# Decoding float64 weights to float32 on one Trainium2 core: a landing offset and a dtype cast in place of shifts and a sign step

## The chip, the cores and the metric

The kernel runs on one core of a Trainium2 chip. The metric is the device time of one execution in microseconds (us). The kernel before was run three times: 883.78 us is the median, 882.27 the lowest and 884.93 the highest. One further execution was profiled; it took 882.62 us.

## The reference

Two stages follow each other. The first is attention in which a query sees only keys of its own hash bucket; the second is a two-layer network with an ELU between its layers (the names say "moe", but there is one pair of matrices and no routing).

```python
# q, k, v: (4, 8, 768, 64) float32; proj: (64, 6) float32
q_bucket = sum over 6 bits of (q @ proj > 0) * 2**bit      # likewise k_bucket
scores = where(q_bucket == k_bucket, q @ k.T / 8, -1e9)
attn_out = softmax(scores) @ v                             # per batch and head
x = attn_out with the heads side by side                   # (3072, 512)
h = x @ w_in                                               # w_in  (512, 2048)
g = where(h > 0, h, exp(min(h, 0)) - 1)
out = g @ w_out                                            # w_out (2048, 512)
```

The inputs q, k, v and proj are float32. The two weight matrices are float64: a float32 array was multiplied by a float64 scalar. No engine of the core computes in float64, so the kernel has to make float32 numbers out of the 64-bit patterns itself.

## The kernel before, in words

**Stages.** The work is cut into eight chunks, one for each half of the 768 queries of each of the four batches. For a chunk the kernel does the attention of four pairs of heads (24 score tiles of 128 queries by 768 keys, numbered s0, s1, ...) and then the network on the 384 tokens of the chunk (16 blocks of 128 hidden columns). The network of a chunk is interleaved on TensorE with the attention of the next chunk. The first chunk has no network beside it: while its attention runs, the weights are loaded and decoded. That is the part which the change touches.

**Attention of a score tile.** TensorE makes the scores in four matmuls (L840) into one of two double banks of PSUM. VectorE takes them out with a clamp and a running maximum (L863). GpSimd makes the bias of the exponential from the maxima of two tiles (L880). ScalarE computes the exponential in place with its sum (L891). In the first chunk TensorE then transposes the tile in float32 (L907, called flip), ScalarE copies that out (L915), and an fp32 matmul with v follows (L991). In later chunks the normalised tile is split into two f16 halves, on ScalarE (L316) and VectorE (L319), and transposed by DMA.

**Weights.** There are 32 tiles of 128 rows by 512 columns, 16 of w_in and 16 of w_out (function weight_ops, tile i in one(i)). Each tile is loaded from DRAM as 128 rows of 4,096 contiguous bytes (L411). It lands in one of three staging slots in the tile U, or in a fourth at the end of the big tile W, the "raw" slot, which is used for every fourth i. A load waits until the decode before it in that slot is done. The result goes to W, at place i + 1 or i + 2. The decode before:

- ScalarE reads the high word of each float64 as a float32 and multiplies it by 2**-112 (L424, "mul").
- VectorE shifts the result left by three bits (L429) and ors in the low word shifted right by 29 (L430, "or"). Without its sign bit this is the float32.
- TensorE adds the high bf16 halves of the magnitudes over the 128 rows with a matrix of ones (L437), accumulated in PSUM over the 16 tiles of a matrix. The largest column sum bounds every weight, which gives the power of two by which the weights are scaled later (L454 and L455).
- VectorE takes the sign from the high word and ors it in (L446, "sgn"). It waits for L437, since the column sums need magnitudes.

When all 16 tiles of a matrix are decoded and its scale is known, each tile is split into two f16 halves (L472 on ScalarE and L475 on VectorE, through the helpers at L316 and L319). The first matmul of the network (L1083) needs that of w_in.

**Order.** A planner (class Plan) gives each step an engine, an estimated duration, a due time and its dependencies, plays the steps through, and emits every engine's instructions in the order that comes out. On the chip each engine and each DMA queue keeps to that order, so a waiting instruction holds what stands behind it. The loads stand on SP's queue, in one row with the loads of q, k and v, the DMA transposes of K and O and small copies of the hash bits (K<-zb, O<-zb). Buffers are rings with a fixed number of slots. `met` is the list of earlier users of the part of W where a decoded tile goes: the end of W first serves as staging for two of the pairs of heads (stages 1 and 2: natk, natq and their q and k), as scratch for the squares of v (junk0), and as the raw slot.

```python
met = [u for a, z, users in regions if a < (place + 1) * SL and place * SL < z for u in users]
if (place + 1) * SL > RAW:
    met += raw_users
...
m = add("A", mul, act(SL) + 40.0, due, [l] + met, use=[t], name=f"w{i}mul")
```

## Time and profile before

| what | value |
| --- | --- |
| median of three runs | 883.78 us (882.27 to 884.93) |
| the profiled execution, its own time | 882.62 us |
| its span, first to last instruction | 880.9 us |
| TensorE (PE) busy in the span | 809.3 us, 92% |
| ScalarE (ACT) busy | 706.3 us, 80% |
| VectorE (DVE) busy | 696.0 us, 79% |
| GpSimd (POOL) busy | 61.9 us, 7% |
| first matmul of the network (L1083) | at 133.9 us |

The profiled execution's own time is 1.72 us more than its span, and 1.16 us less than the median. In the rows of the profile, "PE busy 60.54 (x318)" is the time in which at least one of 318 matmuls ran in that stretch; PEld is the loading of the stationary matrix, which overlaps PE. PEclk is the clock that TensorE was granted, as a share of full speed. "DMA share" is the mean busy share of the 16 DMA engines in the stretch and can come out a little over 1. Names like U, W, natk are tiles of the kernel; L numbers are lines of the kernel before.

### The profile page before, as it was taken

The numbers are of one execution on the slowest core, as the hardware profiler recorded it, in microseconds if no ns is written. First come the engines' busy times: TensorE is split into PE (matmuls) and PEld (weight loads), VectorE is DVE, ScalarE is ACT, GpSimd is POOL, SyncE is SP. The second block draws the span as 40 slices with busy tenths as digits, with TensorE's granted clock in tenths as the row PEclk, the third lists the DMA queues.
The fourth block names the chain that finished last, engine by engine and source line by source line (L and its number), as shares of the span: only waits on it lengthen the run. The fifth ranks groups of instructions, "written<-read, shape, count | busy, mean of one in ns | idle before, by whom it ended". The sixth has DMA issues, their size and how long they took to land. (4 is left out here: it accounts for less than half of the span.)

```text
span 880.9 us, 14721 instructions
## 1 busy us (share of the span) xinstructions
PE 809.3 (92%) x5119; PEld 432.4 (49%) x5119; DVE 696.0 (79%) x1485; ACT 706.3 (80%) x1293; POOL 61.9 (7%) x123
## 2 busy tenths in 40 slices
PE   1676987899999999999999999989999999999997
PEld 0233543444554555545555555545555555555553
DVE  6899999999997777898887777888887777773332
ACT  4567899999988798988888789987987878874443
POOL 1000000000010000000010000000110000000000
PEclk9988899999999999999999999999999999999999
DMA  9967628878896789795977679967976767563001
GB/s 250 286 186 223 195 46 195 167 135 161 142 181 115 139 165 189 166 184 122 191 162 128 121 171 200 189 137 135 170 163 122 134 115 145 103 100 51 36 0 36
DMA packets 367466, 128.98 MB, mean 146 GB/s; under 512 B 342248, under 2 KB 360352, under 8 KB 367392
## 3 DMA queue, kind: packets, MB, share of 16 engines
q1 hardware_dynamic: 367088, 127.91, 69.4%
q8 instruction: 40, 0.66, 0.3%
q14 instruction: 34, 0.28, 0.1%
q10 hardware_dynamic: 304, 0.13, 0.1%
HBM read 35.65 MB, written 6.29 MB: 48 GB/s over the span
## 5 line engine op out<-in xcount | busy, mean ns | idle before, releaser
L1083 PE MATMUL h<-x,W 128*128 128x384 f16 x1536 | 310.6, 326 | 1.0 <-ACT U L1111 0.9
L1135 PE MATMUL o<-W,U 128*128 128x512 f16 x1152 | 307.4, 379 | 1.6 <-DVE U L319 1.2
L891 ACT ACTIVATE pt<-pt,nb,sg 128x768 f32<-128x768 f32 x192 | 195.3, 1018 | 43.0 <-POOL nb L880 42.9
L1083 PEld LDWEIGHTS <-W 128*128 128x128 f16 x1536 | 148.7, 97 | 137.7 <-issue 6.1
L863 DVE TENSOR_SCALAR_CACHE_REDUCE pt<-s 128x768 f32<-128x768 f32 x180 | 171.4, 952 | 27.1 <-PE s L840 13.5
L319 DVE SCALAR_TENSOR_TENSOR hl<-pt,r,hl 128x768 f16<-128x768 f32 x168 | 167.0, 1014 | 15.2 <-ACT hl L316 15.1
L840 PE MATMUL s<-K,O 128*128 128x384 f16 x720 | 150.3, 332 | 14.2 <-DVE pt L863 13.8
L1135 PEld LDWEIGHTS <-U 128*128 128x128 f16 x1152 | 110.0, 97 | 104.7 <-DVE U L319 3.7
L316 ACT ACTIVATE hl<-pt,r 128x768 f16<-128x768 f32 x168 | 149.1, 926 | 5.8 <-issue 2.1
L840 PEld LDWEIGHTS <-O 128*128 128x128 f16 (+1 forms) x768 | 74.1, 100 | 84.4 <-issue 40.1
L880 POOL TENSOR_SCALAR nb<-m,sg 128x2 f32<-128x2 f32 x96 | 58.6, 611 | 725.2 <-DVE pt L863 580.5
L316 ACT ACTIVATE U<-U,sgg 128x384 f16<-128x384 f32 x128 | 77.9, 609 | 36.4 <-DVE U L1114 36.1
L1114 DVE SCALAR_TENSOR_TENSOR U<-U 128x384 f32<-128x384 f32 x128 | 70.7, 553 | 37.3 <-ACT U L1111 37.2
L319 DVE SCALAR_TENSOR_TENSOR U<-U,sgg 128x384 f16<-128x384 f32 x128 | 78.7, 615 | 25.6 <-ACT U L316 24.6
L1107 ACT ACTIVATE U<-h,ch 128x384 f32<-128x384 f32 x128 | 72.7, 568 | 32.3 <-PE h L1083 30.9
L1021 PE MATMUL av<-PT,vhl 128*64 128x384 f16 x1008 | 90.7, 328 | 7.2 <-DMA PT<-hl 6.3
L1021 PEld LDWEIGHTS <-vhl 128*64 128x64 f16 x1008 | 59.1, 110 | 38.2 <-issue 14.8
L1111 ACT ACTIVATE U<-h,ch 128x384 f32<-128x384 f32 x128 | 72.7, 568 | 0.0
L930 DVE TENSOR_SCALAR r<-sm 128x2 f32<-128x2 f32 x84 | 13.8, 165 | 30.6 <-ACT pt L891 30.4
L891 ACT ACTIVATION_READ_ACCUMULATOR pt<-pt,nb,sg 128x1 f32 x192 | 36.2, 188 | 0.0
L907 PE MATMUL flip<-W,pt 128*128 128x128 f32 x144 | 25.5, 313 | 6.4 <-ACT pt L891 3.0
L907 PEld LDWEIGHTS flip<-W,pt 128*128 128x128 f32 x144 | 19.2, 160 | 18.4 <-ACT PT L915 9.4
(118 smaller groups left out, 572.1 us busy)
## 6 DMA issues: line engine op xcount, KB each, us to landing
U<-in_moe_w_in_dram SPq DMA_DIRECT2D x12, 512.0 KB
vf<-in_v_dram SPq DMA_DIRECT2D x16, 384.0 KB
U<-in_moe_w_out_dram SPq DMA_DIRECT2D x12, 512.0 KB
qst<-in_q_dram SPq DMA_DIRECT2D x30, 192.0 KB
kst<-in_k_dram SPq DMA_DIRECT2D x14, 384.0 KB
out_dram<-W SPq DMA_DIRECT2D x16, 256.0 KB
PT<-hl SPq DMA_TRANSPOSE x168
W<-in_moe_w_in_dram SPq DMA_DIRECT2D x4, 512.0 KB
```

The lines of the kernel that those rows point to most:

```text
L316: nc.scalar.activation(o, x, AF.Copy, scale=s)
L319: nc.vector.scalar_tensor_tensor(o, x, s, hi, ALU.mult, ALU.subtract)
L840: nc.tensor.matmul(s.t[:, y, :HALF], O[x][:rows, j * HC + t, :], K[x][:rows, j * NC + y * HC : j * NC + (y + 1) * HC, :].rearrange("p a b ...
L863: nc.vector.tensor_scalar(pt.t.rearrange("p (n e) -> p n e", n=2), s.t[:, :, :HALF], CLAMP, None, ALU.max, ALU.max, accum_out=m.t[:, y : y ...
L880: nc.gpsimd.tensor_scalar(nb.t, m.t, sg_of(n), -1.0, ALU.mult, ALU.mult)
L891: nc.scalar.activation(pt_.t, pt_.t, AF.Exp, bias=nb.t[:, y : y + 1], scale=sg_of(n), accum_out=sm.t[:, z : z + 1])
L1021: nc.tensor.matmul(av.t[j * D : (j + 1) * D], vs["hl"][p].t[:, j, c, vx, :], PTs[j].t[:, :, px, c, :], start=y == 0, stop=y == 3 * NC - 1,)
L1083: nc.tensor.matmul(h.t, WH[:, g * KT + t, wx, fc * P : (fc + 1) * P], xbuf[NP * ci + t].t[:, xx, :], start=t == 0 and y == 0, stop=t == KT ...
L1107: nc.scalar.activation(e.t, h.t, AF.Exp, scale=c["ch"])
L1111: nc.scalar.activation(hp.t, h.t, AF.Relu, scale=c["ch"])
L1114: nc.vector.scalar_tensor_tensor(e.t, e.t, -1.0, hp.t, ALU.add, ALU.min)
L1135: nc.tensor.matmul(banks[t][:, :DO], g16.t[:, gx, t * P : (t + 1) * P], WH[:, NSI + 1 + f, wx, :], start=f == 0 and y == 0, stop=f == NF - ...
```

## The change

A float64 has one sign bit, 11 exponent bits and 52 bits of mantissa. Its upper 16 bits read as a bf16 have the sign, the exponent without its lowest three bits, and then those three bits and four bits of mantissa as the bf16's mantissa. Cast to f16, which has ten mantissa bits and five exponent bits, the same number has the sign, five exponent bits, the three bits, the four bits and three zeros: for numbers of the size of these weights that is the high half of the float32 but for its last three bits. These and the low half are the next 32 bits of the float64, shifted right by 13. To read these 32 bits as one aligned word the tile must lie two bytes further on in SBUF.

So the load now lands at byte 2 of its slot: `in` is the 2,048 16-bit elements from index 1 on, `top` is every fourth bf16, and `low` is every second 32-bit word. GpSimd clears the target in W (new, "zero"). ScalarE casts `top` from bf16 to f16 into the upper halves of the cleared words (in place of "mul"). VectorE shifts `low` right by 13 and ors it in (the one step left of three). The sign comes along with the cast, so no step waits for TensorE any more.

The bound changes with it, since the tile now has its signs: TensorE multiplies each 128 by 128 block of the high bf16 halves, transposed, with itself, and adds all blocks of a matrix up in one 128 by 128 bank. Its diagonal holds sums of squares. The largest entry of each row is taken (128 by 128 instead of 128 by 512), a matmul with ones adds these up over the partitions, and half the exponent of that is the scale (`squares=True`). TensorE now does four matmuls of 128 columns with four loads of weights per tile, in place of one matmul of 512 columns.

Three small things come along. U gets two more columns and the raw slot two more elements for the offset. The weight's place is met (`met`) by the clearing, and no longer by ScalarE's step. In the first chunk the matmuls that spread the inverse sums ("rows") are planned after the chunk's transposes (`after=flips`), and the step that takes these rows (xw) is named to the planner as the next user of the score tile's ring, so that a slot is kept for it.

```diff
-    U = const.tile([P, 3 * 2 * SL], F32, name="U")
+    U = const.tile([P, 3 * 2 * SL + 2], F32, name="U")
...
-    area["U"] = [U[:, i * 2 * SL : (i + 1) * 2 * SL].bitcast(I32).rearrange("p (n x) -> p n x", x=2) for i in range(3)]
+
+    def staged_at(t, at):
+        halves = t.bitcast(I16)[:, 2 * at : 2 * at + 4 * SL + 4]
+        return {
+            "in": halves[:, 1 : 1 + 4 * SL],
+            "low": t.bitcast(I32)[:, at : at + 2 * SL].rearrange("p (n x) -> p n x", x=2)[:, :, 1],
+            "top": halves[:, 4:].bitcast(BF16).rearrange("p (n x) -> p n x", x=4)[:, :, 0],
+        }
+
+    area["U"] = [staged_at(U, i * 2 * SL) for i in range(3)]
...
-    area["raw"] = [spare(SL, 2).bitcast(I32)]
+    area["raw"] = [staged_at(flat(spare(1, 2 * SL + 2)), 0)]
...
-                nc.sync.dma_start(flat(t.t), src)
+                nc.sync.dma_start(t.t["in"], src)
...
-            def mul():
-                nc.scalar.activation(d, t.t[:, :, 1].bitcast(F32), AF.Copy, scale=2.0**-112)
-
-            m = add("A", mul, act(SL) + 40.0, due, [l] + met, use=[t], name=f"w{i}mul")
-
-            def bits_():
-                nc.vector.tensor_scalar(di, di, 3, None, ALU.logical_shift_left)
-                nc.vector.scalar_tensor_tensor(di, t.t[:, :, 0], 29, di, ALU.logical_shift_right, ALU.bitwise_or)
-
-            s = add("V", bits_, vec(SL, 2.0) + vec(SL) + 70, due, [m], use=[t], name=f"w{i}or")
+            def zero():
+                nc.gpsimd.memset(d, 0.0)
+
+            def top_():
+                nc.scalar.activation(d.bitcast(F16).rearrange("p (n x) -> p n x", x=2)[:, :, 1], t.t["top"], AF.Copy)
+
+            def join():
+                nc.vector.scalar_tensor_tensor(di, t.t["low"], 13, di, ALU.logical_shift_right, ALU.bitwise_or)
+
+            z = add("G", zero, 600.0, due - 4, met, name=f"w{i}zero")
+            m = add("A", top_, act(SL) + 40.0, due, [l, z], use=[t], name=f"w{i}top")
+            s = decoded[i] = add("V", join, vec(SL), due, [m], use=[t], name=f"w{i}or")
 
             def bound():
                 if i in (0, NSI):
-                    acc["t"] = ps_o.tile([P, 512], F32, tag="o2", name="acc")[:, :SL]
-                nc.tensor.matmul(
-                    acc["t"], ones, d.bitcast(BF16).rearrange("p (n t) -> p n t", t=2)[:, :, 1],
-                    start=i in (0, NSI), stop=i in (NSI - 1, NSI + NSO - 1),
-                )
-
-            b = add("P", bound, 220.0, due - 40, [s, cleared] + ([maxes[0]] if i == NSI else []), after=bounds[o][-1:], late=160.0, name=f"w{i}sum")
+                    acc["t"] = ps_o.tile([P, 512], F32, tag="o2", name="acc")[:, :P]
+                high = d.bitcast(BF16).rearrange("p (n t) -> p n t", t=2)[:, :, 1]
+                for x in range(SL // P):
+                    part = high[:, x * P : (x + 1) * P]
+                    nc.tensor.matmul(
+                        acc["t"], part, part, start=i in (0, NSI) and x == 0,
+                        stop=i in (NSI - 1, NSI + NSO - 1) and x == SL // P - 1,
+                    )
+
+            b = add("P", bound, 400.0, due - 40, [s] + ([maxes["seen"]] if i == NSI else []), after=bounds[o][-1:], late=160.0, name=f"w{i}sum")
             bounds[o].append(b)
-
-            def sign():
-                nc.vector.scalar_tensor_tensor(di, t.t[:, :, 1], -(2**31), di, ALU.bitwise_and, ALU.bitwise_or)
-
-            decoded[i] = add("V", sign, vec(SL), due, [b], use=[t], name=f"w{i}sgn")
             if raw:
-                raw_users.append(decoded[i])
+                raw_users.append(s)
             if i in (NSI - 1, NSI + NSO - 1):
+                av = buf("av")
 
                 def reduce_():
                     nc.vector.tensor_reduce(wst["m2"][:, o : o + 1], acc["t"], axis=AX.X, op=ALU.max)
-                    wst["ex", o], wst["sc", o] = exponents(wst["m2"][:, o : o + 1], 1, 2.0**-17, W_TOP, f"w{o}", const)
+
+                def sum_():
+                    av.t = sum_over(wst["m2"][:, o : o + 1], 1)
+
+                def scale():
+                    wst["ex", o], wst["sc", o] = exponents(av.t, 1, 2.0**-34, W_TOP, f"w{o}", const, squares=True)
                     if o == 1:
                         wst["e2"] = const.tile([P, 1], F32, name="we2")
                         nc.vector.tensor_tensor(wst["e2"], wst["ex", 0], wst["ex", 1], ALU.mult)
 
-                maxes[o] = add("V", reduce_, vec(SL) + 5 * TINY, due, [b], name=f"wmax{o}")
+                r = maxes["seen"] = add("V", reduce_, vec(P), due - 40, [b], name=f"wmax{o}")
+                q_ = add("P", sum_, 60.0, due - 40, [r, filled_ones], new=[av], late=160.0, name=f"wsum{o}")
+                maxes[o] = add("V", scale, 6 * TINY, due - 40, [q_], use=[av], name=f"wscale{o}")
...
-            a2 = add("P", spread, 1400.0, due - 1, [a1, cleared], new=[rb], use=[rw], late=160.0, name=f"rows{n}")
+            a2 = add("P", spread, 1400.0, due - 1, [a1, cleared], after=flips, new=[rb], use=[rw], late=160.0, name=f"rows{n}")
-            a3 = add("A", take, act(HALF, 1), due - 1, [a2, vs["scaled"]], new=[xw], use=[rb], name=f"xw{n}")
+            a3 = pt.heir = add("A", take, act(HALF, 1), due - 1, [a2, vs["scaled"]], new=[xw], use=[rb], name=f"xw{n}")
```

The planner is given the new steps, and the engines' orders come out differently. Lines of the changed kernel stand up to 19 further down: L863 is L881 there, L880 is L898, L319 is L329, L720 is L738, L430's place is taken by L440, L437's by L452 and the clearing is L434.

VectorE, from the scale of the third pair of heads (sg) on, before. W<-W,qks is the f16 split of that pair's k and q, zb<-z,pjt its neighbour's hash bits, and the last row is the first score tile's maximum:

```order
L430 SCALAR_TENSOR_TENSOR W<-U,W 128x512
L319 SCALAR_TENSOR_TENSOR W<-W,qks 128x12x64
L319 SCALAR_TENSOR_TENSOR W<-W,qks 128x6x64
L720 TENSOR_SCALAR zb<-z,pjt 128x384
L663 COPY W<-W 128x6x64
L446 SCALAR_TENSOR_TENSOR W<-U,W 128x512
L429 TENSOR_SCALAR W<-W 128x512
L430 SCALAR_TENSOR_TENSOR W<-U,W 128x512
L720 TENSOR_SCALAR zb<-z,pjt 64x384
L772 TENSOR_REDUCE vx_335<-vx 128x1
L446 SCALAR_TENSOR_TENSOR W<-U,W 128x512
L863 TENSOR_SCALAR pt,m<-s 128x768
```

The same place in the changed kernel, from sg up to the second score tile's maximum (pt,m<-so):

```order
L618 SCALAR_TENSOR_TENSOR sg<-ke 128x1
L881 TENSOR_SCALAR pt,m<-s 128x768
L329 SCALAR_TENSOR_TENSOR W<-W,qks 128x12x64
L329 SCALAR_TENSOR_TENSOR W<-W,qks 128x6x64
L738 TENSOR_SCALAR zb<-z,pjt 128x384
L681 COPY W<-W 128x6x64
L440 SCALAR_TENSOR_TENSOR W<-U,W 128x512 x2
L440 SCALAR_TENSOR_TENSOR W<-W 128x512
L738 TENSOR_SCALAR zb<-z,pjt 64x384
L440 SCALAR_TENSOR_TENSOR W<-U,W 128x512
L881 TENSOR_SCALAR pt,m<-so 128x768
```

The first maximum has moved from behind the split, the hash bits and the steps of two to three weight tiles to directly behind the scale, and a weight tile has one row (L440) where it had three.

GpSimd, from the end of the set-up to the end, before. nb is the bias of the exponential, one row for two score tiles:

```order
L337 MEMSET W 128x128
L338 ISA
L338 AFFINE_SELECT W<-W 128x128
L880 TENSOR_SCALAR nb<-m,sg 128x2 x96
L1253 UNCONDITIONAL_BRANCH
```

And in the changed kernel, where L434 clears a weight tile's place:

```order
L347 MEMSET W 128x128
L348 ISA
L348 AFFINE_SELECT W<-W 128x128
L434 MEMSET W 128x512 x22
L898 TENSOR_SCALAR nb<-m,sg 128x2
L434 MEMSET W 128x512
L898 TENSOR_SCALAR nb<-m,sg 128x2 x2
L434 MEMSET W 128x512 x6
L898 TENSOR_SCALAR nb<-m,sg 128x2 x9
L434 MEMSET W 128x512 x3
L898 TENSOR_SCALAR nb<-m,sg 128x2 x84
L1272 UNCONDITIONAL_BRANCH
```

The 32 clearings stand in GpSimd's one queue with the biases: 22 ahead of the first bias, one behind it, six ahead of the fourth, and the last three behind the twelfth.

More of the change, by code (lines that the diff above doesn't have):

```diff
@@ L11 @@
 I32 = mybir.dt.int32
+I16 = mybir.dt.int16
 AF = mybir.ActivationFunctionType
@@ L382, in lsh_attention_moe @@
     filled_ones, cleared, proj_top, projected = begin_ops()
-    wi64 = w_in.bitcast(I32)
-    wo64 = w_out.bitcast(I32)
+    wi64 = w_in.bitcast(I16)
+    wo64 = w_out.bitcast(I16)
     decoded, split_done = {}, {}
@@ L403, in one @@
                 g, kt = i // KT, i % KT
-                src = wi64[kt * P : (kt + 1) * P, 2 * g * SL : 2 * (g + 1) * SL]
+                src = wi64[kt * P : (kt + 1) * P, 4 * g * SL : 4 * (g + 1) * SL]
             else:
@@ L817, in pair_ops @@
         PTs = []
-        filled = []
+        filled, flips = [], []
         sums = buf("sw") if whole else None
@@ L920, in pair_ops @@
                         eye_users.append(fl)
+                        flips.append(fl)
                         ev = add(
```

## The prediction

> **What bounds the kernel now.** I read the page first, for the busy shares and the chain of work that ended last. PE is busy for 92% of the span, and the chain, followed back from the end, is almost all PE, in the two matmuls of the network.
>
> ```profile
> span 880.9 us, 14721 instructions
> PE 809.3 (92%) x5119; PEld 432.4 (49%) x5119; DVE 696.0 (79%) x1485; ACT 706.3 (80%) x1293; POOL 61.9 (7%) x123
> PE o L1135 6%; PE h L1083 6%; PE av L1021 1%; PE s L840 1%; ACT pt L891 0%; DVE W L1189 0%; DVE pt L863 0%; DVE U L319 0%; ACT U L316 0%; ACT U L1107 0%; DVE U L1114 0%; DVE po L1173 0%; ACT U L1111 0%; ACT po L1169 0%; DVE r L930 0%
> ```
>
> An average over stages hides what matters here, so next come the busy times by stretch. I chose the cuts at the points where the limiting engine changes.
>
> ```profile
> core 0: us, PE busy (x) PEld busy (x) DVE busy (x) ACT busy (x) POOL busy (x), PEclk, DMA share, GB/s
> 10.00:30.00 20.00, 8.61 (x41) 2.56 (x41) 18.85 (x52) 11.22 (x24) 0.00 (x0) 1.00 1.05 300
> 30.00:110.00 80.00, 60.54 (x318) 32.98 (x318) 72.81 (x164) 56.35 (x113) 3.73 (x10) 0.89 0.69 206
> 110.00:130.00 20.00, 16.37 (x122) 9.52 (x121) 19.62 (x49) 20.00 (x44) 0.55 (x2) 1.00 0.16 33
> 130.00:240.00 110.00, 98.07 (x637) 51.52 (x634) 104.51 (x217) 108.19 (x196) 8.23 (x15) 1.00 0.81 159
> 240.00:870.00 630.00, 619.84 (x3983) 333.41 (x3982) 475.51 (x990) 502.28 (x905) 46.11 (x69) 1.00 0.69 135
> 870.00:881.00 11.00, 5.41 (x25) 2.09 (x23) 2.41 (x4) 2.72 (x5) 0.00 (x0) 0.91 0.20 72
> ```
>
> From 240 us on PE is busy 619.84 of 630 us: there the kernel is as long as its matmuls. From 110 to 240 us ACT has 128.19 of 130 us, with DVE close behind. From 10 to 110 us DVE is busy 91.66 of 100 us, while PE has 69.15 and ACT 67.57. That is the first chunk's attention with the weights decoded beside it, and only there does DVE alone set the pace. What the first chunk takes less, everything behind it starts sooner; nothing behind it gets shorter by itself.
>
> The decode lies in that stretch: the sign step's last instruction starts at 120.5 us, the network's first matmul at 133.9.
>
> ```profile
> L446 DVE SCALAR_TENSOR_TENSOR W<-U,W x24: 675/686/710, 23.2 to 120.5; 128x512 int32<-128x512 int32 x24
> L1083 PE MATMUL h<-x,W x1536: 322/326/337, 133.9 to 870.3; 128*128 128x384 f16 x192
> ```
>
> **The change part by part.** The groups that the change touches (busy us, mean ns of one, idle before):
>
> ```profile
> L430 DVE SCALAR_TENSOR_TENSOR W<-U,W 128x512 int32<-128x512 int32 x24 | 16.6, 692 | 0.8
> L446 DVE SCALAR_TENSOR_TENSOR W<-U,W 128x512 int32<-128x512 int32 x24 | 16.3, 687 | 1.0 <-PE acc L437 1.0
> L424 ACT ACTIVATE W<-U 128x512 f32<-128x512 f32 x24 | 15.9, 668 | 13.9 <-DMA U<-in_moe_w_in_dram 11.7 <-DMA U<-in_moe_w_out_dram 2.2
> L437 PE MATMUL acc<-W,ones 128*128 128x512 bf16 x32 | 14.4, 470 | 6.3 <-DVE W L430 5.9
> L429 DVE TENSOR_SCALAR W<-W 128x512 int32<-128x512 int32 x32 | 13.5, 422 | 2.2 <-ACT W L424 2.2
> L437 PEld LDWEIGHTS <-ones 128*128 128x128 bf16 x32 | 3.3, 109 | 5.9 <-issue 5.5
> ```
>
> *DVE.* The or step stays as one step of the same form, two words in and one out, 692 ns. The shift (422 ns) and the sign (687 ns) go: 1.11 us for each of 32 tiles, 35.5 us. By stretch (10 to 30, 30 to 110, 110 to 130 us), L446 first and L429 second:
>
> ```profile
> 10.00:30.00 20.00, 2.07 (x3) 1.00 1.05 300
> 30.00:110.00 80.00, 17.42 (x26) 0.89 0.69 206
> 110.00:130.00 20.00, 2.08 (x3) 1.00 0.16 33
> ...
> 10.00:30.00 20.00, 1.66 (x4) 1.00 1.05 300
> 30.00:110.00 80.00, 10.54 (x25) 0.89 0.69 206
> 110.00:130.00 20.00, 1.28 (x3) 1.00 0.16 33
> ```
>
> That is 3.7, 28.0 and 3.4 us. DVE's work from 30 to 110 us falls from 72.8 to 44.9 us, below both PE and ACT, so DVE stops being the bound.
>
> *ACT.* The cast reads 512 elements at the same distance of eight bytes as the multiplication and writes 512, four bytes apart. I take L424's 668 ns: no change. Bounds are 0.1 us less or more on each tile, 3 us either way.
>
> *PE.* Each tile streams 512 columns as before, in four pieces, and loads four stationary blocks where it loaded one. Lower bound: nothing, as loads run beside matmuls (from 240 us on PEld has 333 us inside a PE that is hardly ever idle). Upper bound: three more loads of 109 ns bare, 0.33 us a tile. I take 0.1, nearer to the hidden end: 26 tiles from 30 to 110 us make 2.6 us. Their wait for DVE remains (5.9 us in 12 waits before), but DVE no longer waits for them.
>
> *POOL.* Not in the trace at this size. Two rows bound it:
>
> ```profile
> L329 POOL MEMSET W<- 128x384 f16 x2 | 0.8, 417 | 0.0
> L337 POOL MEMSET W<- 128x128 f32 x1 | 0.2, 209 | 0.1
> ```
>
> From 128 to 384 elements the price rises by 208 ns, so 512 elements cost some 520 ns; 32 of them 16.7 us, on an engine with 3.73 of 80 us in use. The cover is POOL's idleness. What can be late is what is queued behind a clearing that waits: the bias, and behind it the exponential.
>
> ```profile
> 4.28 0.29 POOL L338 TENSOR_SCALAR_AFFINE_SELECT W<-W 128x128 f32<-128x128 f32 x1
> 16.55 1.56 SPq L668 DMA_TRANSPOSE O<-W  x1
> 23.30 1.44 PE L840 MATMUL s<-K,O 128*128 128x384 f16 x4
> 30.35 0.19 ACT L313 ACTIVATION_READ_ACCUMULATOR W<-vf 128x1 f32 x1
> 31.24 0.95 DVE L863 TENSOR_SCALAR_CACHE_REDUCE pt<-s 128x768 f32<-128x768 f32 x1
> ```
>
> The first 18 clearings write unused places and run from 4.6 to 14 us; four more wait for the staging of the second pair of heads, whose last reader is the transpose issued at 16.55 us, so they end by some 22 us if it lands two us later. The first bias needs two score tiles, the first of which is only computed at 23.3 us. The clearing behind the first bias waits for the squares of v, over at 30.5 us, which stand ahead of the first exponential on ACT as well. I cost POOL at nothing.
>
> *Start.* The first score tile is ready at 24.7 us, and its maximum runs at 31.24, behind the split and weight steps that the order shows. Now it stands in front of them; that work must still be done before the second maximum, so I count not the 6.5 us but the 3.7 that DVE loses up to 30 us. The loads set the rest of that stretch (DMA share 1.05).
>
> *Sum.* From 30 to 110 us PE is the next bound, with 60.5 + 2.6 = 63.1 us, and ACT has 56.4. DVE as the bound reached 72.81 of 80 us, 91%, through queues in fixed order. With the same share, PE needs 63.1 / 0.91 = 69.3 us: 10.7 less. From 110 to 240 us ACT is the bound and its work stays: nothing. From 240 us on PE: nothing. Together 3.7 + 10.7 = 14.4 us. The profiled execution took 882.62 us (its span and 1.72), so 868.2; I say 868. That execution lies 1.16 us below the median of the three runs, inside their spread.
>
> *DMA and its landing.* Two bytes off is the part for which no row stands. The tiles go through these issues and two like them for w_out, 32 in all:
>
> ```profile
> U<-in_moe_w_in_dram SPq DMA_DIRECT2D x12, 512.0 KB
> W<-in_moe_w_in_dram SPq DMA_DIRECT2D x4, 512.0 KB
> ```
>
> 32 times 524,288 bytes are 16.8 MB, which at the 300 GB/s of the row with the engines full take 56 us. All DMA work from 10 to 110 us is 20 x 1.05 + 80 x 0.69 = 76 us. I take the landing at its old speed, as rows of 4,096 contiguous bytes stay such rows.
> A rule speaks against that. The Trainium skill (DMA: Bandwidth & Descriptors, "How a descriptor splits into AXI transactions") says that a descriptor is cut at 256-byte boundaries, so one that starts off a boundary needs one transaction more. If it holds for the landing side too, a row makes 17 transactions in place of 16, an estimate of 6% or 3.5 us of DMA time; no run here shows it yet. The sum stays the same by it, and it lowers the chance of the rival below.
>
> **The rivals.**
>
> *The odd landing is slow (slower than before).* If each weight row takes x times as long, the DMA engines have 76 + 56 (x - 1) us of work for that stretch. At x = 1.16 that is the 85 us that my sum leaves of the hundred; at 1.43 the whole gain is gone; at 2 it is 132 us, 32 more than now, and 915 us comes out. For it: ACT waited 11.7 us for w_in even before, and SP's one queue holds the transposes behind the loads. Against it: bytes and contiguous runs are unchanged.
>
> *ACT alone is the bound.* PE ran at 0.89 of its clock from 30 to 110 us; at full clock its 60.5 us are 54, less than ACT's 56.35. At the 98.6% that ACT reaches from 110 to 240 us (128.19 of 130), the stretch takes 57.1 us, 22.9 less, and with the start 26.6: 856 us. Against it: flips and their copies go back and forth between PE and ACT through two banks.
>
> *The queues hold each other up.* If the next bound reaches only 80% of the stretch, since three engines of like load pass each tile on in turn, PE needs 78.9 us: 1.1 plus 3.7 less, 878 us. The waits for it are there:
>
> ```profile
> ACT pt L891 <- POOL nb L880: 10.6, 3, 4.9
> PE acc L437 <- DVE W L430: 5.9, 12, 1.1
> ```
>
> *Clearings hold DVE.* The copies at L640 and L663 move 512 elements in less time than the others (1536 in 545 ns), and 9 of them lie from 10 to 110 us (L640 first, then L663, each from 10 and from 30 us on). If each meets a clearing and waits for it, that is 9 x 0.52 = 4.7 us on a path, 873 us.
>
> ```profile
> L640 DVE COPY K<-K 64x1536 f16<-64x1536 f16 x16 | 8.7, 545 | 1.0 <-DMA K<-natk 1.0
> ...
> 10.00:30.00 20.00, 1.09 (x2) 1.00 1.05 300
> 30.00:110.00 80.00, 1.09 (x2) 0.89 0.69 206
> ...
> 10.00:30.00 20.00, 0.75 (x3) 1.00 1.05 300
> 30.00:110.00 80.00, 0.50 (x2) 0.89 0.69 206
> ```
>
> The Trainium skill (SBUF — State Buffer, "Who interferes with whom") has the rule for it: a VectorE copy in a two-port mode and a GpSimd instruction lock each other out of a shared port pair. No row shows such a meeting yet; the one step of the decode in such a mode, by its 422 ns, is the one removed.
>
> **How the numbers follow.** Forecast 0.62; ACT alone 0.12; queues hold each other up 0.12; clearings 0.05; slow landing 0.09. Same means within 0.3%, 2.6 us, about what a measurement of this kernel tells from no change. The queue case gives 5 us and its worse half can fall inside that: 0.05 for the same. Faster is 0.62 + 0.12 + 0.05 + 0.07 = 0.86, slower 0.09. The range runs from ACT alone, 856, to the queue case, 878; outside lie the slow landing and the worse half of the queue case, with the tail beyond ACT's floor some 0.16.
>
> **What would show it.** Right: DVE has 1.1 us less for each tile, its busy share from 30 us on falls to some 65% until the network begins, PE's rises over 85%, the first h matmul starts near 119.5 us and the stretch behind it keeps its length. Wrong: the cast takes over 0.8 us; L424's 13.9 us of idle time before it, which loads ended, become tens; the bias starts late behind L434; or the first h matmul is early and the end is not, because ACT's stretch to 240 us grew.

## The result, and the profile after

| | median | range | executions |
| --- | --- | --- | --- |
| before | 884.29 us | 882.27 to 887.97 | 13 |
| after | 878.87 us | 874.31 to 881.83 | 13 |

The ratio is 0.9929, 95% interval [0.9909, 0.9949]: 6.3 us faster (4.5 to 8.0), where the prediction said 14.4. The profiled execution of the changed kernel took 875.86 us. Its page and its busy times by stretch, cut as before (columns: stretch, its length, PE, PEld, DVE, ACT, POOL busy, PE's clock, DMA share, GB/s):

```profile
span 874.1 us, 14875 instructions
PE 803.9 (92%) x5217; PEld 433.7 (50%) x5217; DVE 670.7 (77%) x1423; ACT 707.8 (81%) x1293; POOL 81.8 (9%) x155
```

```profile
10.00:30.00 20.00, 6.15 (x36) 2.33 (x39) 17.56 (x52) 8.48 (x17) 5.16 (x11) 1.00 0.82 218
30.00:110.00 80.00, 64.08 (x488) 38.49 (x490) 57.93 (x136) 71.39 (x144) 9.80 (x22) 0.96 0.76 236
110.00:130.00 20.00, 17.79 (x125) 10.12 (x118) 18.70 (x48) 19.84 (x39) 1.74 (x2) 1.00 0.38 92
130.00:240.00 110.00, 96.11 (x606) 48.67 (x604) 98.98 (x204) 103.25 (x187) 10.31 (x13) 0.95 0.79 151
240.00:870.00 630.00, 619.47 (x3976) 333.80 (x3974) 472.41 (x985) 500.68 (x901) 46.05 (x69) 1.00 0.69 133
```

Two things stand out beside the rows of before. From 30 to 110 us VectorE has made room (57.93 of 80 us instead of 72.81) and ScalarE is now the busiest, with 71.39. And from 130 to 240 us, where the changed steps no longer run, all three engines are less busy than before (ScalarE 103.25 instead of 108.19 of 110 us): time is lost there that no engine's work accounts for (the window holds other work than before, as the network starts sooner).

The changed steps themselves, as groups (busy us, mean ns of one, idle before):

```profile
L437 ACT ACTIVATE W<-U 128x512 f16<-128x512 bf16 x24 | 18.6, 785 | 3.6 <-DMA U<-in_moe_w_in_dram 3.1 <-DMA U<-in_moe_w_out_dram 0.5
L440 DVE SCALAR_TENSOR_TENSOR W<-U,W 128x512 int32<-128x512 int32 x24 | 16.3, 686 | 12.8 <-ACT W L437 12.7
L434 POOL MEMSET W<- 128x512 f32 x32 | 15.5, 538 | 15.6 <-DMA O<-W 8.3 <-DVE W L329 5.3 <-ACT W L323 1.1
L452 PE MATMUL acc<-W 128*128 128x128 bf16 x128 | 13.2, 238 | 7.8 <-DVE W L440 7.8
```

The join costs what the or cost, the clearing 538 ns where some 520 were estimated, the products no more than the matmul with the ones (13.2 us for all, 14.4 before). The cast is dearer, 785 ns against 668. The waits of ScalarE for the loads of w_in fell from 11.7 to 3.1 us.

To see where the gain went I follow the first matmuls of the network in the trace. The first h matmul starts at 122.2 us:

```profile
L1102 PE MATMUL h<-x,W x1536: 322/326/527, 122.2 to 863.6; 128*128 128x384 f16 x192
```

It was 133.9, so 11.7 us are gained there. The 193rd h matmul starts the second chunk's share; it came at 241.0 before and comes at 236.2 now, 4.8 earlier. Between these two matmuls PE starts the same 621 matmuls, tile for tile (the rows count those under way at an edge too), yet they take 114.0 us where they took 107.1. The rows for that stretch, of before and of after:

```profile
133.90:241.00 107.10, 95.17 (x624) 50.11 (x622) 101.61 (x212) 105.62 (x193) 6.97 (x14) 1.00 0.81 158
```

```profile
122.20:236.20 114.00, 98.98 (x624) 50.34 (x622) 102.94 (x213) 107.14 (x194) 11.00 (x14) 0.96 0.76 150
```

So 6.9 us are given back behind the point up to which I had counted: PE is busy for 3.8 us more with the same matmuls, at a lower clock, and idle for 3.1 us more. Not all of it is lost for good. Up to the 385th h matmul, the start of the third share and again the same work for PE, the rows of before and of after are:

```profile
133.90:337.50 203.60, 188.80 (x1231) 100.77 (x1229) 180.77 (x378) 185.89 (x338) 14.94 (x26) 1.00 0.81 156
```

```profile
122.20:329.10 206.90, 191.78 (x1231) 100.27 (x1229) 181.30 (x376) 187.19 (x339) 18.34 (x26) 0.98 0.79 152
```

The second share alone takes 92.9 us where it took 96.6, so some 3.6 of the 6.9 us come back in it, and 3.3 are lost.

Another loss lies at the start. After, then before (start us, duration us):

```profile
4.53 8.47 POOL L434 MEMSET W<- 128x512 f32 x18
5.45 0.15 DVE L606 TENSOR_SCALAR qkm<-qkx 128x1 f32<-128x1 f32 x1
5.63 7.39 DVE L608 TENSOR_SCALAR ke<-qkm 128x2 int32<-128x2 int32 x1
13.71 0.17 DVE L608 TENSOR_SCALAR ke<-qkm 128x2 int32<-128x2 int32 x1
```

```profile
5.56 0.17 DVE L590 TENSOR_SCALAR ke<-qkm 128x2 int32<-128x2 int32 x1
```

A VectorE step of two columns, 0.17 us before, now ends at 13.02 us, when the row of 18 clearings ends at 13.00. The step of one column just ahead of it took its usual 0.15 us in the middle of that row, and the same step at 13.71, behind the row, is back at 0.17.

### The profile page after: what moved, and what is told of

Same layout as the page of the kernel before. It is cut to its first block, busy times and chain, and to the rows that moved or that the text cites. A ratio compares the mean times of both kernels' runs of the same rounds, so it can differ in the third digit from the quotient of the medians.

```text
span 874.1 us, 14875 instructions
## 1 busy us (share of the span) xinstructions
PE 803.9 (92%) x5217; PEld 433.7 (50%) x5217; DVE 670.7 (77%) x1423; ACT 707.8 (81%) x1293; POOL 81.8 (9%) x155
## 5 line engine op out<-in xcount | busy, mean ns | idle before, releaser
L881 DVE TENSOR_SCALAR_CACHE_REDUCE pt<-s 128x768 f32<-128x768 f32 x180 | 171.2, 951 | 28.1 <-PE s L858 15.0
L329 DVE SCALAR_TENSOR_TENSOR hl<-pt,r,hl 128x768 f16<-128x768 f32 x168 | 166.0, 1013 | 10.7 <-ACT hl L326 10.6
L1154 PEld LDWEIGHTS <-U 128*128 128x128 f16 x1152 | 110.2, 98 | 112.9 <-ACT U L326 8.2
L898 POOL TENSOR_SCALAR nb<-m,sg 128x2 f32<-128x2 f32 x96 | 63.1, 657 | 683.0 <-DVE pt L881 568.9
L329 DVE SCALAR_TENSOR_TENSOR U<-U,sgg 128x384 f16<-128x384 f32 x128 | 78.6, 614 | 25.9 <-ACT U L326 24.5
L329 DVE SCALAR_TENSOR_TENSOR x<-av,x 128x384 f16<-128x384 f32 x28 | 15.5, 554 | 14.7 <-ACT x L326 14.7
```

The lines of the kernel that those rows point to most:

```text
L329: nc.vector.scalar_tensor_tensor(o, x, s, hi, ALU.mult, ALU.subtract)
L881: nc.vector.tensor_scalar(pt.t.rearrange("p (n e) -> p n e", n=2), s.t[:, :, :HALF], CLAMP, None, ALU.max, ALU.max, accum_out=m.t[:, y : y ...
L898: nc.gpsimd.tensor_scalar(nb.t, m.t, sg_of(n), -1.0, ALU.mult, ALU.mult)
L1154: nc.tensor.matmul(banks[t][:, :DO], g16.t[:, gx, t * P : (t + 1) * P], WH[:, NSI + 1 + f, wx, :], start=f == 0 and y == 0, stop=f == NF - ...
```

## The experiments

In the table "h0" is the start of the first h matmul, "stretch" the time from there to the 193rd and "385th" the start of that matmul, all in us, read from one profiled execution of each; "clock" is PE's in the stretch. Up to the 193rd and the 385th PE has done the same matmuls of attention and network in every run. Up to h0 too, but for l_v16, which has by then done 12 score matmuls more (some 4 us at 332 ns), and j_beforev, which has done four fewer: their h0 and stretch don't compare with the others as they stand.

| kernel | ratio to before, interval | h0 | stretch | 385th | clock |
| --- | --- | --- | --- | --- | --- |
| before | 1 | 133.9 | 107.1 | 337.6 | 1.00 |
| after | 0.9929 [0.9909, 0.9949] | 122.2 | 114.0 | 329.1 | 0.96 |
| a_repeat | 0.9910 [0.9891, 0.9930] | 121.7 | 112.6 | 327.2 | 0.95 |
| b_columns | 0.9885 [0.9864, 0.9905] | 119.2 | 113.0 | 325.1 | 0.95 |
| c_twice | 0.9862 [0.9838, 0.9886] | 120.1 | 113.3 | 326.3 | 0.95 |
| d_noclear | 0.9863 [0.9838, 0.9889] | 119.6 | 114.2 | 326.7 | 0.96 |
| e_bias | 0.9869 [0.9850, 0.9887] | 119.1 | 113.0 | 324.9 | 0.95 |
| f_vsplit | 0.9833 [0.9815, 0.9851] | 120.3 | 110.2 | 323.6 | 0.98 |
| h_oldorder | 0.9999 [0.9985, 1.0013] | 130.6 | 111.4 | 335.3 | 0.97 |
| n_oldplan | 0.9969 [0.9951, 0.9988] | 133.6 | 107.7 | 335.9 | 0.98 |
| m_vonly | 0.9886 [0.9861, 0.9911] | 123.6 | 108.2 | 324.9 | 1.00 |
| l_v16 | 0.9829 [0.9802, 0.9855] | 121.6 | 105.9 | 320.8 | 0.98 |
| k_vbias | 0.9870 [0.9840, 0.9899] | 118.3 | 111.1 | 322.5 | 0.98 |
| j_beforev | 1.0084 [1.0052, 1.0116] | 138.5 | 112.1 | 346.2 | 0.97 |

**a_repeat**, the changed kernel once more, for the spread between executions.

> The changed kernel once more, nothing edited. It is the base of this batch and shows how far one execution's profile stands from another's. In the first profile of the changed kernel the integer step on the scale at L608 (128x2) took 7.39 us, and it ended at 13.02 us, where the 18 clearings on GpSimd that began at 4.53 us ended. Theory A (the clearings hold that step, and it costs the start some 5 us that the end gets to see): the same 7.4 us, and the first K transpose at 15.5 us. Theory B (a chance event of one execution): under 1 us. By both, a time of 876 to 882 us.

The step is held for 7.05 us again and the stretch is 112.6 us. Both losses belong to the kernel, not to one execution; the stretch can differ by 1.4 us between executions.

**b_columns** takes the lock away: the scale steps of the first four pairs do one column at a time.

```diff
-            nc.vector.tensor_scalar(
-                ex.t.bitcast(I32), mall.bitcast(I32), 1, 0x7F800000, ALU.logical_shift_right, ALU.bitwise_and
-            )
+            cols = [slice(y, y + 1) for y in range(n)] if early else [slice(0, n)]
+            for y in cols:
+                nc.vector.tensor_scalar(
+                    ex.t[:, y].bitcast(I32), mall[:, y].bitcast(I32), 1, 0x7F800000, ALU.logical_shift_right, ALU.bitwise_and
+                )
...
-            nc.vector.tensor_scalar(sc.t, sc.t, 2.0 ** (QK_TOP - 64), None, ALU.mult)
+            for y in cols:
+                nc.vector.tensor_scalar(sc.t[:, y], sc.t[:, y], 2.0 ** (QK_TOP - 64), None, ALU.mult)
```

> For the first four pairs of heads the steps on the scale of shape 128x2 (L608 and the one after the reciprocal) are done one column at a time, 128x1, like the step at L606 just before, which took 0.15 us amid the clearings. The clearings stay. Theory A (the clearings hold the 128x2 step and the whole start hangs on it): no step at L608 over 0.6 us, the first K transpose is issued near 11 us in place of 15.5, the first h matmul comes 3 to 5 us earlier than in the unedited changed kernel, and the time is 3 to 5 us less. Theory B (the start has slack, since the loads set its pace, and the gain that is missing is lost after the network begins): the first h matmul moves by under 1.5 us and the time by under 1 us. Theory C (start matters for the first h matmul, but the stretch after it gives it back): first h matmul 3 to 5 us earlier, time within 1.5 us.

```profile
4.52 4.72 POOL L434 MEMSET W<- 128x512 f32 x10
6.27 0.27 DVE L610 TENSOR_SCALAR ke<-qkm 128x1 int32<-128x1 int32 x2
```

```profile
119.20:232.20 113.00, 99.05 (x622) 50.39 (x620) 102.90 (x212) 106.92 (x193) 10.92 (x14) 0.95 0.76 151
```

Inside the same row of clearings, two steps of one column take 0.27 us together. h0 comes at 119.2 us, 3.0 earlier than after and 2.5 earlier than a_repeat: the lock is confirmed, and without it the front is as early as forecast (119.5). The stretch stays at 113.0: the give-back is another matter.

**c_twice** makes every clearing twice, **d_noclear** none (the cast then writes whole f32 words).

```diff
                 nc.gpsimd.memset(d, 0.0)
+                nc.gpsimd.memset(d, 0.0)
```

> Each clearing on GpSimd is done twice; all else, the order on the engines included, is as in the changed kernel. The 18 at the start then last some 17 us in place of 8.47. Theory A: the step at L608 ends near 21.5 us in place of 13.0, the first K transpose is issued near 24 us, and the first h matmul and the end come 6 to 8 us later. Theory B: GpSimd is idle for 9 tenths of the time and the start has slack: under 1.5 us. Theory C: the first h matmul 6 to 8 us later, the end under 3 us later.

```diff
-                nc.gpsimd.memset(d, 0.0)
+                pass
...
-                nc.scalar.activation(d.bitcast(F16).rearrange("p (n x) -> p n x", x=2)[:, :, 1], t.t["top"], AF.Copy)
+                nc.scalar.activation(d, t.t["top"], AF.Copy)
```

> The clearings are left out, and ScalarE writes its cast as 512 float32 over the whole word instead of 512 f16 into upper halves, so that no step reads an uncleared word; the weights come out with a wrong exponent. VectorE, TensorE and the loads are as in the changed kernel. It takes away everything that GpSimd does for the decode, and shows whether writing every second 16 bits is what makes the cast 0.78 us in place of the 0.67 of the multiplication before. Theory A: start as before the change (first K transpose at 10.6 us), first h matmul 4 to 6 us earlier than in the changed kernel, time 4 to 6 us less. Theory B: under 1.5 us. Theory C: first h matmul 4 to 6 us earlier, time within 2 us. The cast: 0.67 us if the 16-bit steps cost, else 0.78.

Doubling came out faster than the changed kernel (872.96 us against 877.20 for a_repeat, beside it), against every expectation. The rows of c_twice show why:

```profile
4.52 0.53 POOL L434 MEMSET W<- 128x512 f32 x1
5.11 0.52 POOL L435 MEMSET W<- 128x512 f32 x1
5.57 0.53 POOL L434 MEMSET W<- 128x512 f32 x1
5.78 0.34 DVE L609 TENSOR_SCALAR ke<-qkm 128x2 int32<-128x2 int32 x1
```

The second clearing of a place waits for the first, so the clearings no longer run as one row, and the step of two columns gets through at 6.12 us, when the one clearing under way ends. What locks VectorE out is the row without a gap, not the amount of clearing. In d_noclear, with no clearing there, the step takes 0.17 us with both columns, and the cast takes 674 ns again:

```profile
5.85 0.17 DVE L608 TENSOR_SCALAR ke<-qkm 128x2 int32<-128x2 int32 x1
...
L437 ACT ACTIVATE W<-U 128x512 f32<-128x512 bf16 x24 | 16.0, 674 | 7.1 <-DMA U<-in_moe_w_in_dram 6.1 <-DMA U<-in_moe_w_out_dram 0.7
```

Without clearings and with the cheaper cast, 32 times 0.11 or 3.5 us of ScalarE, h0 stands where b_columns has it (119.6 and 119.2). So neither the dearer cast nor what GpSimd does after the start costs anything that these runs can tell.

**e_bias** looks at the stretch. In after, the second part of it has these rows:

```profile
186.60 3.13 POOL L898 TENSOR_SCALAR nb<-m,sg 128x2 f32<-128x2 f32 x1 [8.58 <-DVE pt L881]
186.66 0.84 ACT L323 ACTIVATE natk<-vf 128x768 bf16<-128x768 f32 x1
189.77 1.03 ACT L909 ACTIVATE pt<-pt,nb,sg 128x768 f32<-128x768 f32 x1 [2.17 <-POOL nb L898]
190.79 0.83 ACT L323 ACTIVATE natk<-vf 128x768 bf16<-128x768 f32 x1
192.27 4.02 PE L1154 MATMUL o<-W,U 128*128 128x512 f16 x9 [4.02 <-ACT U L326]
193.20 0.83 ACT L323 ACTIVATE natk<-vf 128x768 bf16<-128x768 f32 x1
194.15 0.84 ACT L323 ACTIVATE natk<-vf 128x768 bf16<-128x768 f32 x1
```

The bias takes 3.13 us (mean 657 ns), ScalarE waits 2.17 for it, and all four squares of v (L323) of the next pair stand in ScalarE's queue within 7.5 us, so that the half of the network's activation that PE needs comes late and PE stands for 4.02 us. Before, these squares lay at 168.1, 173.9, 185.9 and 195.6 us. e_bias is b_columns with twelve biases given to VectorE.

```diff
-                nc.gpsimd.tensor_scalar(nb.t, m.t, sg_of(n), -1.0, ALU.mult, ALU.mult)
+                eng = nc.vector if NT <= G < 2 * NT else nc.gpsimd
+                eng.tensor_scalar(nb.t, m.t, sg_of(n), -1.0, ALU.mult, ALU.mult)
```

> b_columns with the bias of the second chunk's twelve score tiles computed by VectorE instead of GpSimd (12 steps of 128x2), order unchanged. Theory that the held biases are part of the give-back: the 3.13 us row of the bias at 186 us is gone (0.1 to 0.2 us on VectorE), the stretch from the first h matmul to the 193rd gets 2 to 3 us shorter, 110 to 111 us, and the time is 872 to 873 us. Rival: the wait only moves (the maximum is late, or the exponential waits for other work on ScalarE): 113 us, 874.8 us within 1.

PE's gap there shrinks from 4.03 us in b_columns to 1.77, but the stretch is 113.0 us, as in b_columns to the tenth. Taking the bias off GpSimd gains nothing, with VectorE 1.4 us busier in the stretch for it: the held bias alone was not what the stretch hung on.

**f_vsplit** is b_columns with the splits of v in the second chunk planned earlier, and with them their loads and squares.

```diff
-            due = s0 + 2 * HC * p if b else NT + 2 * HC * p
+            due = s0 + 2 * HC * p if b else NT + 2 * HC * p - 8
```

> b_columns with the due time of the second chunk's v splits 8 score tiles earlier, so that the planner sets the loads and squares of v sooner and further apart. Theory that v's clumped squares make part of the give-back: ScalarE's row of squares at 187 to 195 us is spread, the stretch from the first h matmul to the 193rd takes 109 to 111 us, and the time is 871 to 873 us. Rival (no single place; ScalarE at its limit): 113 us, 874.8 us within 1.5; or the earlier splits delay the first h matmul, seen as a start later than 119.5 us.

```profile
157.20 0.83 ACT L323 ACTIVATE natk<-vf 128x768 bf16<-128x768 f32 x1
165.07 0.84 ACT L323 ACTIVATE natk<-vf 128x768 bf16<-128x768 f32 x1
174.67 0.83 ACT L323 ACTIVATE natk<-vf 128x768 bf16<-128x768 f32 x1
184.59 0.84 ACT L323 ACTIVATE natk<-vf 128x768 bf16<-128x768 f32 x1
```

```profile
120.30:230.50 110.20, 96.65 (x623) 49.81 (x620) 101.74 (x212) 105.66 (x193) 8.80 (x14) 0.98 0.78 155
```

The squares are spread over 27 us, PE's gap of 4 us and the half clock behind it are gone, and the stretch is 2.8 us shorter than in b_columns; 2.4 of these are less busy time of PE (96.65 against 99.05 us). At the 385th h matmul this kernel is some 14 us ahead of before, its whole gain at h0 (13.6) and a little more. The ratio 0.9833 is 14.8 us (13.2 to 16.4). That is the size of the forecast, but for a kernel with two more edits.

**h_oldorder and n_oldplan** keep the planner's graph of the kernel before and write the new instructions in the old places. The edit of h_oldorder against the kernel before, cut to the decode steps; both also do the scale steps one column at a time:

```diff
...
             def mul():
-                nc.scalar.activation(d, t.t[:, :, 1].bitcast(F32), AF.Copy, scale=2.0**-112)
+                nc.gpsimd.memset(d, 0.0)
+                nc.scalar.activation(d.bitcast(F16).rearrange("p (n x) -> p n x", x=2)[:, :, 1], t.t["top"], AF.Copy)
...
             def sign():
-                nc.vector.scalar_tensor_tensor(di, t.t[:, :, 1], -(2**31), di, ALU.bitwise_and, ALU.bitwise_or)
+                pass
...
```

> The new instructions in the old order: the planner works on the graph of the kernel before, so everything stands in its old place; the clearing and the cast are written where the multiplication stood, the join where shift and or stood, the four products of the tile where the matmul with the ones stood, nothing where the sign step stood. The scale steps take one column at a time, as in b_columns. Theory (the new plan's order behind the network's start gives back some 6 us: v's squares in a clump, late loads of q and v, a bias that is held): the stretch from the first h matmul to the 193rd is 107 us as before, not 113, and if the first h matmul stays near 119.5 us the time is 868 to 870 us, ratio 0.981 to 0.984. Rival (that stretch is longer whatever the order, from the clock or from work that is left over): 113 us again, and a time within 1.5 us of 874.8, ratio 0.988. Third possibility: the old order leaves the first chunk waiting in its old places and the first h matmul comes at 125 us or later, with a stretch of 107 us; then the time is about 874 us again, but for another reason.

Here the order was the old one only up to about 120 us, so that the first sentence of the expectation holds for the front alone; behind, v's squares stood at 194.8, 195.9, 199.8 and 201.1 us, a clump again, and the stretch was 111.4. n_oldplan moves the two words, and the old order holds to the end: on ScalarE and on SP's queue the trace has the instructions of before one for one.

```diff
-    W = const.tile([P, NSI + NSO + 2, SL], F32, name="W")
+    Wf = const.tile([P, (NSI + NSO + 2) * SL + 2], F32, name="W")
+    W = Wf[:, : (NSI + NSO + 2) * SL].rearrange("p (s e) -> p s e", e=SL)
```

> h_oldorder once more, mended: there the staging place at the end of the weights' tile was two words longer, which moved the staging of the later pairs by two words into one more weight's place, added dependencies, and so the planner left the old order at about 120 us. Here the tile itself is two words longer and every queue has the order of the kernel before to the end, with the new instructions in the old places and the scale steps one column at a time. Theory (the give-back comes from the new plan's order, v's squares in a clump above all): with the squares spread as before, the stretch from the first h matmul to the 193rd takes 107 us within 1 and PE's clock stays at 0.98 or more in it; the first h matmul comes at 130 us as in h_oldorder, so the time is 880 to 884 us, ratio 0.993 to 0.997. Rival (the new instructions lengthen that stretch whatever the order): 111 us or more, ratio 1.000 again.

```profile
30.00:110.00 80.00, 60.60 (x394) 37.68 (x394) 48.16 (x116) 56.40 (x111) 15.04 (x34) 0.87 0.69 204
133.60:241.30 107.70, 96.41 (x623) 50.15 (x620) 102.07 (x212) 105.62 (x192) 7.32 (x14) 0.98 0.79 159
```

```profile
DVE W L439 <- ACT W L434: 18.1, 10, 4.7
```

The stretch is 107.7 us, as before, with the new instructions in place: the give-back comes from the order. It does not come from an early start of the network as such, for two kernels that start it late have long stretches in other orders: h_oldorder (130.6 and 111.4 us) and j_beforev below (138.5 and 112.1 us, some 1.3 of it its four score matmuls), which even has the old instructions. The front shows the order's part as well. VectorE has 48.16 of 80 us there, 24.6 less than before, and h0 comes at 133.6 us, where it was. The time freed became a wait for ScalarE's cast, 18.1 us in ten waits, where it was 2.2 for the multiplication: as long as ScalarE and the loads keep their places, nothing comes sooner. (The new order has such waits too, 12.7 us in the row of L440 above, but ScalarE gets 71.39 us of work done in these 80 us, and here 56.40.) The run is 0.3% faster all the same; in its trace 1.7 us of that stand at the 385th h matmul. So the new order makes the front's gain, and gives part of it back behind. The two hints to the planner that came with the change (`after=flips` and the heir), put into the kernel before, leave its order as it was; what they do to the order of the changed kernel no run here shows.

**m_vonly** is f_vsplit's due time with the lock left in, **l_v16** goes 16 score tiles earlier, **k_vbias** is f_vsplit with e_bias, **j_beforev** the kernel before with f_vsplit's edit; the edit of l_v16, the others being shown above:

```diff
-            due = s0 + 2 * HC * p if b else NT + 2 * HC * p
+            due = s0 + 2 * HC * p if b else NT + 2 * HC * p - 16
```

> The changed kernel with the earlier due time of f_vsplit alone; the scale steps of the first four pairs take both columns again. Theory (the start's lock and the give-back are two losses of their own): the 128x2 step is held for 7 us again, the first h matmul comes some 3 us later than in f_vsplit, at 123 us, the stretch to the 193rd stays at 110 us and the time is 874 us, ratio 0.986. Rival (the give-back follows from the front's time, so a later front has less of it): as fast as f_vsplit, 871.6 us within 1.

> f_vsplit with the due time of the second chunk's v splits 16 score tiles earlier instead of 8. Theory (what the new plan gives back is a matter of where v's work stands, and 8 was enough to spread it): within 1.5 us of f_vsplit's 871.6, or slower because the earlier splits stand ahead of the weights and the first h matmul comes later than 120.3 us, at 122 us or so. Rival (more is to be had in the same direction): 869 us or less, with the stretch to the 193rd h matmul under 109 us.

> f_vsplit with the second chunk's twelve biases on VectorE as well, as in e_bias, order unchanged. Theory (the held bias only mattered together with the clump of squares): no more than 1 us either way from f_vsplit, 871.6 us, ratio 0.982 to 0.9845. Rival (each takes its own part of the give-back): 870 us or less, ratio under 0.982.

> A control: the kernel before, with only the due time of the second chunk's v splits moved 8 score tiles earlier, as in f_vsplit. Theory (f_vsplit takes back what the new plan gave away): before has no such clump, so nothing is gained, ratio 0.997 to 1.003, and the stretch from the first h matmul to the 193rd stays at 107 us within 1. Rival (f_vsplit is an improvement of its own that has nothing to do with the change): ratio 0.994 to 0.997, some 3 to 4 us faster.

```profile
5.78 7.22 DVE L608 TENSOR_SCALAR ke<-qkm 128x2 int32<-128x2 int32 x1
```

In m_vonly the step is held for 7.22 us again, h0 comes 3.3 us later than in f_vsplit, and the ratio is 0.0053 worse: in the times, lock and give-back are two losses that add up. Its stretch, expected at 110 us, is 108.2; PE has a gap of 2.22 us in both kernels, and in f_vsplit alone the clock falls to half behind it (134.7 to 138.1 us, 1.7 us of work), so that difference need not come from the later front. In l_v16 the stretch is 105.9 us, but 12 of its score matmuls stand ahead of h0; with them it would be some 110, an estimate, as in f_vsplit. The time is f_vsplit's within the intervals; it is the fastest, 15.2 us under before, with f_vsplit level. k_vbias was expected within 1 us of f_vsplit and came out 3.3 us slower in ratio, with intervals that overlap: no gain from the biases in either pairing. The control was expected to do nothing and made the kernel before 7.4 us slower. So the edit is no gain of its own; but it also shows that a new order alone is worth several us either way, and that spread squares (here at 177 to 205 us) do not make a good stretch by themselves. f_vsplit, too, is a new order as a whole: that the clump and nothing else of it was what cost there is argued from the rows, not shown.

## Why the prediction was wrong

*The front, 14.4 us: right in size, in part by luck.* With the lock away h0 comes 14.7 us earlier, and at 119.2 us where 119.5 was said. The reason was only half right. VectorE was the busiest engine there, but n_oldplan takes the same steps off it and gains nothing at h0: the gain needs the planner to pull ScalarE's work and the loads forward. The next bound was ScalarE, at 71.39 of 80 us or 89%, not PE, at 80%; a sum over PE's work at 91% came near by chance.

*"From 110 to 240 us ACT is the bound and its work stays: nothing."* This is the step that failed. ScalarE's work in the stretch stayed (105.62 and 107.14 us), but the stretch grew by 6.9 us with the planner's new order, which put the next chunk's v work in a clump; PE then stood, and its clock fell. I took work for time; the 98.6% that ScalarE had reached were a property of the old plan. The text had named this as what would make it wrong. n_oldplan shows that the order is the cause. Of the 6.9 us, 3.8 are PE's busy time at a lower clock and 3.1 its idle time; f_vsplit takes back 2.8, most of them by the clock; the 3.1 by which its stretch is still longer than before I have not traced to one place. "From 240 us on PE: nothing" was off the other way: the second share, which begins near there, is 3.6 us shorter and makes up for half. PE is idle for 0.1 us of it, where it was for 2.9; why, I have not traced.

*"I cost POOL at nothing."* This failed too: the first clearings hold a VectorE step for 7.4 us, worth 2.5 to 3.0 us at h0, and 2.2 to 4.7 us of the time (a_repeat against b_columns, m_vonly against f_vsplit). The rival "clearings hold DVE" had the mechanism, but at the copies of L640 and L663 with one clearing each; it was one small step behind eighteen. In sum: 14.7 - 3.0 - 6.9 = 4.8 us at the 193rd h matmul, 8.5 at the 385th, and 6.7 at the last. The last 1.8 us say little, since they are no more than two executions of the changed kernel differ by (534.5 us from the 385th to the last in after, 536.9 in a_repeat).

*The cast*, taken at 668 ns with 0.1 us either way, took 785: outside, though not by much. It cost nothing (d_noclear). *PE* at 0.1 us a tile: it was nothing, 13.2 us for 14.4. *The landing two bytes off* was right to be priced at its old speed: the 4,096 rows of 4,096 bytes are packets of their own in the traces, and one took 159 ns in the median in both (188 ns in the mean before, 182 after). Against the Trainium skill's rule (DMA: Bandwidth & Descriptors, "How a descriptor splits into AXI transactions"), by which a row would need a seventeenth transaction if the rule held for the landing side, no 6% are seen.

## What to carry to other kernels

Removing work from the busiest engine moves the end only if the order lets the others come forward: with a planner, write the new instructions into the old order once, and compare; that parts the change from the new plan. Behind the point where the work ends, look for the same work taking longer, with milestones such as the first, the 193rd and the 385th matmul of one kind; count that the work between them is the same, and take a later one too, since what one stretch loses the next can win back. Do not let GpSimd run a row of clearings without gaps beside VectorE steps like the one of 128x2 that was held here, or do such steps one column at a time.

## What the runs showed of the hardware

A row of 18 clearings on GpSimd held one VectorE step of 128x2 for 7.39 us, to its end, while steps of 128x1 passed at 0.15. The Trainium skill (SBUF — State Buffer, "Who interferes with whom") says of GpSimd and of a VectorE instruction in a two-port mode that the one who issues first has the shared ports for its whole instruction; c_twice agrees (0.34 us, to the end of the clearing under way), but the row of after goes further: the step did not get in between two clearings of a row.

PE's clock fell after a gap of its own (2 us each, the changed kernel):

```profile
188.00:190.00 2.00, 0.25 (x2) 0.00 (x0) 2.00 (x3) 0.23 (x1) 1.73 (x1) 1.00 0.37 98
190.00:192.00 2.00, 0.00 (x0) 0.00 (x0) 0.55 (x2) 2.00 (x5) 0.00 (x0) 0.63 1.13 354
192.00:194.00 2.00, 1.73 (x5) 0.59 (x6) 1.29 (x2) 2.00 (x5) 0.00 (x0) 0.50 1.11 222
194.00:196.00 2.00, 2.00 (x6) 0.71 (x5) 0.23 (x2) 1.97 (x6) 0.00 (x0) 0.50 0.66 122
196.00:198.00 2.00, 2.00 (x10) 1.02 (x9) 1.46 (x8) 1.60 (x4) 0.00 (x0) 0.67 0.00 0
198.00:200.00 2.00, 2.00 (x14) 1.07 (x11) 1.97 (x5) 2.00 (x4) 0.78 (x1) 1.00 0.00 0
```

PE stands from 188.2 to 192.3 us, is granted half its clock until some 197, and the slowest h matmuls of the run, at 196.4 and 196.8, take 527 ns instead of 326. The Trainium skill (TensorE: Matmul & The Clock Gate, "What's actually happening") tells of such a halving after an idle window of about 3.4 us; the 0.50 agrees, but shorter gaps brought it too: 2.51 us from 153.7 in this trace (half the clock from 156.4 to 159.8) and 2.22 us in f_vsplit, while one of 2.22 us in m_vonly did not (clock 1.00 in the table). The stall so costs more than its own length: PE's busy time in the stretch is 98.98 us for work that took 95.17 before.
